# Scores of four heads packed on the rows of the TensorE array, with one exp for the four, in a kernel planned at build time

## The chip, the cores and the metric

The kernel runs on one core of a Trainium2 chip. The metric is the device time of one execution in microseconds (us); three runs of the kernel before took 340.61, 340.77 and 341.06 us, median 340.77. The profile is of one further execution, whose span from first to last instruction is 337.3 us.

## The reference

Two independent computations on bf16 inputs share the launch, and their outputs lie side by side in one result.

- Part A (2048 tokens, 640 channels): a causal convolution of k with four taps, times v, gives kv; kv is convolved along all 2048 tokens with a long filter per channel (by FFT in the reference), `ssm_D * kv` is added, and the sum is multiplied by q.
- Part B (2048 tokens, 640 channels, 32 heads of width 20): attention with a memory, over four segments of 512 tokens.

```python
for s in range(N):                                   # N = 4 segments of L = 512
    logits = einsum('bhqd,bhkd->bhqk', qs, ks) * scale + mask      # causal
    a_dot = einsum('bhqk,bhkd->bhqd', softmax(logits), vs)
    num = einsum('bhld,bhde->bhle', phi(qs), M)      # phi(t) = t + 1 if t > 0 else exp(t)
    den = einsum('bhld,bhd->bhl', phi(qs), z)[..., None] + 1e-06
    outs.append(g * num / den + (1.0 - g) * a_dot)
    M = M + einsum('bhld,bhle->bhde', phi(ks), vs)
    z = z + einsum('bhld->bhd', phi(ks))
```

q, k and v are x times three 640 x 640 weights; the heads' outputs are multiplied by a fourth.

## The kernel before, in words

**Part A** (`a_chunks`) runs five times, for 128 channels each. The long convolution is done as Fourier transforms by matmuls: filter and kv are transformed (`fwd`, banks "a", copied to F by ACT), combined by sums and products on DVE (`bfly`, `pointwise`, `ybfly`: tiles Xh, Kh, S, pr), and transformed back (`inverse`). `kshift` makes the four taps on PE.

**Part B** runs in eight units u: segment s = u // 2, half = u % 2 of 16 heads. `b_proj_chunks` multiplies x by the weights (banks "b"), copies K, Q and V out by ACT, and transposes K and Q by DMA, so that KT and QT hold four heads on the partitions: head hl has rows 32 hl to 32 hl + 19, and a group g of four heads is one slice. Row 32 hl + 20 holds ones in KT and a bound in QT that keeps the exponents small (`bound`). In each token tile of segments 0 to 2, phi of K is made (ACT exp into xm, two DVE ops into PK, lines 714 to 716), and `mem` updates the memory matrix Mbd from PK and V: the product is multiplied by a block mask, its last column by a second factor em (lines 747 and 748), and added (749).

`b_attn_chunks` does the attention. A matmul over 128 rows of KT would mix four heads, so `spread` (line 775) first copies each head's 21 rows of KT by a DMA on the GpSimd queue into KZ, a tile that is zero elsewhere: KZ[:, g, hl] holds head hl on its own rows and zeros on the others. `attn` (782) then goes through a group's heads in two pairs. For each of three specifications of key blocks (block 0; blocks 1 and 3 in one bank; block 2) it makes the scores of both heads, each with 128 rows of KZ against QT, into one "st" bank per head, and ACT takes the exp of each bank into ET: twelve exps a group, of 512, 512 and 256 elements per head. Only queries at or after the key block are computed. DVE multiplies the diagonal blocks by the causal mask in two ops (line 804), PE multiplies ET by V and phi(Q) by Mbd into the "o" bank, in two halves of the queries (805), and DVE divides (820, 827) and adds the two parts into o_s (830), once per half. `outt`, `outproj` and, for the last segment, `out_last` transpose o_s by DMA and multiply by the output weights.

**What sets the order.** All operations are recorded first, with the engine they run on, the PSUM bank they use and their predecessors; a planner (`plan`, `forward`, `backward`, lines 239 to 431) then lays them out by a list schedule with prices written in `price` (182), due times by chunk from two tables of offsets (BIAS, HOLD, from line 879), and hands out the banks: three "st", two "a", two "b", one "o" (878). Every engine gets its instructions in this fixed order (`emit`, line 433), and waits only for what each one needs. So all profile lines carry line 438, the call that emits, and are told apart by their tiles.

Of the kernel before, what the change touches and what calls it, by code (L numbers as in the profile page):

```python
# [26 lines left out]
ET_OFF = {0: 0, 1: 512, 3: 896, 2: 1024}  # L27
# [66 lines left out]
class Recorder:  # L94
# [13 lines left out]
    def bank(self, kind):  # L108
        i = self.turn[kind] % len(self.slots[kind])
        self.turn[kind] += 1  # L110
        t = self.slots[kind][i]
        b = self.home[t[:].tensor.name] = Bank(kind, t[:].tensor.name)
        b.row = kind if kind in ("st", "o") else self.key[0] if kind == "b" and self.key[0] == "P" else None
        if b.row:
            b.seq = self.rows.get(b.row, 0)
            self.rows[b.row] = b.seq + 1
        return t
# [17 lines left out]
    def add(self, eng, method, args, kw):  # L135
# [27 lines left out]
        self.price(op, method, outs[0], ins)  # L163
# [18 lines left out]
    def price(self, op, method, out, ins):  # L182
        n = int(np.prod(list(out.shape)[1:]))
        two = lambda a: mybir.dt.size(a.dtype) == 2
        if method == "matmul":
            op.dur += max(n / 2.4 + 2.5, 27.0)
# [42 lines left out]
    def finish(self):  # L229
        for o in self.ops:  # L230
            o.dur, o.lat = int(round(o.dur)), int(round(o.lat))
            o.dma = None if o.dma is None else int(round(o.dma))
            if o.new and o.bank.kind == "a":
# [213 lines left out]
class K3:  # L447
    def __init__(self, ctx, tc, A_q, A_k, A_v, A_shift_k, A_ssm_k, A_ssm_D, B_x, B_wq, B_wk, B_wv, B_wo, B_beta, out):
# [12 lines left out]
        for kind, n in BANKS.items():  # L461
            self.rec.add_banks(kind, [psum.tile([128, 512], f32, name=f"{kind}{i}") for i in range(n)])
# [37 lines left out]
        self.KQ = [c.tile([128, 2, 16, 32], bf16, name=f"KQ{i}") for i in range(2)]  # L500
# [3 lines left out]
        self.NZ = 2  # L504
        self.KZ = [c.tile([128, 2, 4, L], bf16, name=f"KZ{i}") for i in range(self.NZ)]
        for i in range(self.NZ):
            nc.gpsimd.memset(self.KZ[i][:], 0.0)
        self.PqT = [c.tile([128, 4, L], bf16, name=f"PqT{i}") for i in range(2)]
        self.Mbd = [[c.tile([128, 4, 4, VW], bf16, name=f"Mbd{h}{i}") for i in range(2)] for h in range(2)]
        for i in range(2):  # L510
            nc.gpsimd.memset(self.KQ[i][:, :, :, DH:32], 0.0)
            nc.gpsimd.memset(self.KQ[i][:, 0, :, DH:DH + 1], 1.0)
# [5 lines left out]
    def beta_setup(self):  # L518
# [13 lines left out]
        self.emg = em[:].rearrange("p (g h) -> p g h", h=4)  # L532
# [14 lines left out]
    def a_chunks(self, dp):  # L547
# [13 lines left out]
        def turn(c):  # L561
            def f():
                ps = self.bank("a")
# [23 lines left out]
        def kshift(b):  # L587
            def f():
                kr, vt = st["kr"], st["vt"]
                ps = self.bank("a")  # L590
# [8 lines left out]
        def fwd(kind, c):  # L599
            def f():  # L600
# [3 lines left out]
                for i in range(2):  # L604
                    pf = self.bank("a")
# [28 lines left out]
        def pointwise(b):  # L634
            def f():
# [5 lines left out]
                for i in range(2):  # L641
# [3 lines left out]
                    else:  # L645
                        shp = [128, 2, 8, 128]
                        pr = self.ring("pr", shp)
                        V.tensor_tensor(out=pr[:], in0=Xv[:, i:i + 1, :, 0, :].to_broadcast(shp), in1=Kv[:, :, :, 1, :], op=ALU.mult)
                        V.tensor_tensor(out=Sh[:, i, :, :, 1, :], in0=Sh[:, i, :, :, 1, :], in1=pr[:], op=ALU.add)
# [17 lines left out]
        def inverse(c):  # L667
            def f():
                U, qd = st["U"], st["qd"]
                outa = self.ring("outa", [128, 4, 128], n=2)  # L670
                py = self.bank("a")
# [14 lines left out]
    def b_proj_chunks(self, u):  # L686
# [10 lines left out]
        def proj(tci):  # L697
            def f():
                xT = self.xTs[s]
                tok = slice(128 * tci, 128 * tci + 128)  # L700
                KQ = self.KQ[tci % 2]
                for i in range(3):
                    kq = self.bank("b")
# [4 lines left out]
                if tci == 0:  # L708
                    self.KTs[u] = self.ring("KT", [128, 4, L])
                nc.sync.dma_start_transpose(out=self.KTs[u][:, :, tok], in_=KQ[:, 0, :, :])  # L710
                nc.sync.dma_start_transpose(out=QT[:, :, tok], in_=KQ[:, 1, :, :])
                if s < NS - 1:
                    xm = self.ring("xm", [128, 2, 16, DH])
                    nc.scalar.activation(out=xm[:, 0], in_=KQ[:, 0, :, 0:DH], func=ACTF.Exp)
                    V.tensor_scalar(out=xm[:, 1], in0=KQ[:, 0, :, 0:DH], scalar1=1.0, scalar2=1.0, op0=ALU.add, op1=ALU.max)
                    V.tensor_tensor(out=self.PK[:, tci, :, 0:DH], in0=xm[:, 0], in1=xm[:, 1], op=ALU.min)
            return f

        def bound():
# [11 lines left out]
            pb = self.bank("b")  # L731
# [6 lines left out]
        def mem():  # L738
            src, dst = self.Mbd[half][s % 2], self.Mbd[half][(s + 1) % 2]
            pm = self.bank("b")  # L740
# [5 lines left out]
            mt = self.ring("xm", None)[:].rearrange("p a h d -> p (a h d)")[:, 0:352].rearrange("p (g h e) -> p g h e", g=4, h=4)  # L746
            V.tensor_tensor(out=mt[:, :, :, 0:DH + 1], in0=pmv[:, :, :, 0:DH + 1], in1=self.maskbd[:, None, :, 0:DH + 1].to_broadcast([128, 4, 4, DH + 1]), op=ALU.mult)
            V.tensor_tensor(out=mt[:, :, :, DH], in0=mt[:, :, :, DH], in1=self.emg[:, 4 * half:4 * half + 4, :], op=ALU.mult)
# [12 lines left out]
    def o_pieces(self, s, f0, q0):  # L761
        if s < NS - 1:
            return [(self.o_s[s][:].rearrange("p t h d -> p t (h d)")[:, q0:q0 + 2, f0:f0 + 80], 0, 80)]
        low, high = self.o_parts(s)
        cut = min(max(512 - f0, 0), 80)
        return ([(low[:, q0:q0 + 2, f0:f0 + cut], 0, cut)] if cut else []) + ([(high[:, q0:q0 + 2, f0 + cut - 512:f0 + 80 - 512], cut, 80)] if cut < 80 else [])

    def b_attn_chunks(self, u):
# [6 lines left out]
        def spread(gg):  # L775
            def f():
                for hl in range(4):
                    rows = slice(32 * hl, 32 * hl + DH + 1)
                    nc.gpsimd.dma_start(out=self.KZ[gg][rows, :, hl, :], in_=self.KTs[u][rows, 2 * gg:2 * gg + 2, :])
            return f  # L780

        def attn(g):
            def f():
                KZ = self.KZ[g // 2]
# [3 lines left out]
                ET = self.ring("ET", [128, 4, 1280], n=2)  # L788
                for hp in range(2):
                    for spec in (((0, 0),), ((1, 0), (3, 384)), ((2, 0),)):  # L790
                        sts = [self.bank("st") for j in range(2)]
                        width = 0
                        for j in range(2):
                            hl = 2 * hp + j
                            for (kc, c0) in spec:
                                n = L - 128 * kc
# [209 lines left out]
```

## Time and profile before

| from | what | value |
|---|---|---|
| timed runs | median of three | 340.77 us |
| page, 1 | span | 337.3 us |
| page, 1 | POOL (GpSimd) busy | 77.4 us, 23% |
| groups | scores (all four forms) on PE | 512 matmuls, mean 303 ns, 109.4 us busy |
| groups | exps on ACT | 384, mean 642 ns, 193.4 us busy |
| groups | KZ from KT, issued by POOL | 64 DMAs, 39.6 us busy, 148.8 us idle before |
| waits | POOL for PE st before a KZ copy | 104.6 us in 16 waits |
| page, 3 | DMA queue of POOL (q0) | 7.44 MB, 9.6% of 16 engines' span |

A group's line gives the engine, the operation, what it writes and from what, its shape, the count, then busy time and the mean of one in ns, and behind the second bar the engine's idle time just before these instructions with what ended it. Busy time is a union: where two records of an engine overlap, the time counts once. So a mean is longer than the time after which the next instruction can begin. A busy share near 100% of a stretch says that the engine had little to give there; a share of the whole span mixes start, middle and end.

### The profile page before, as it was taken

How to read it: one execution, taken by the hardware profiler on the slowest of the kernel's cores; microseconds unless marked ns; L12 is line 12 of the kernel's file. 1: busy time of each engine (PE TensorE's matmuls, PEld its weight loads, DVE VectorE, ACT ScalarE, POOL GpSimd, SP SyncE). 2: the span in 40 equal slices, each digit the busy share in tenths (PEclk: the TensorE clock that was granted, in tenths of full speed). 3: DMA queues.
4: the chain of work that ended last, by engine and by line, in shares of the span. 5: the costliest groups of instructions: out<-in, count | busy, mean ns of one | idle time of the engine just before them, and what ended most of it. 6: DMA issues, size and time to landing. Idle time of an engine off the chain costs nothing.

```text
span 337.3 us, 9126 instructions
## 1 busy us (share of the span) xinstructions
PE 303.2 (90%) x3546; PEld 222.1 (66%) x3546; DVE 295.0 (87%) x540; ACT 283.7 (84%) x649; POOL 77.4 (23%) x123
## 2 busy tenths in 40 slices
PE   1998789989998699999997999999989999799882
PEld 1676567648876477878774687777755767566651
DVE  0177999999898999999999899999989998999952
ACT  1857469996998899999999999998998999769911
POOL 9322300241003120233020410340021300822210
PEclk9999799999999799999997999999997999999999
DMA  7986995983259456572475156464330352423153
GB/s 227 251 173 141 182 207 153 180 158 70 48 112 200 74 141 107 95 154 73 77 128 136 35 104 96 71 142 93 76 62 18 85 102 53 100 83 87 52 109 93
DMA packets 100186, 38.34 MB, mean 114 GB/s; under 512 B 92160, under 2 KB 97312, under 8 KB 99888
## 3 DMA queue, kind: packets, MB, share of 16 engines
q1 hardware_dynamic: 94816, 30.01, 45.2%
q0 software_dynamic: 4896, 7.44, 9.6%
q8 instruction: 27, 0.44, 0.5%
q10 hardware_dynamic: 432, 0.34, 0.3%
q14 instruction: 15, 0.12, 0.1%
HBM read 13.36 MB, written 5.24 MB: 55 GB/s over the span
## 4 chain that ended last, share of the span: by engine, by line
PE 60%; ACT 15%; DMA 12%; DVE 9%; issue 4%; SPq 0%; DVEq 0%; ACTq 0%
PE b L438 20%; PE a L438 17%; PE st L438 15%; ACT ET L438 10%; PE o L438 7%; DMA QT<-KQ 6%; DMA kr<-in_A_k_dram 2%; ACT F L438 2%; DMA sk<-in_A_ssm_k_dram 2%; DVE S L438 2%; DVE tq L438 2%; DMA oT<-o_s 1%; DVE ET L438 1%; DVE o L438 1%; ACT KQ L438 1%
## 5 line engine op out<-in xcount | busy, mean ns | idle before, releaser
L438 ACT ACTIVATE ET<-st 128x512 bf16<-128x512 f32 (+1 forms) x384 | 193.4, 642 | 6.8 <-PE st L438 6.1
L438 PE MATMUL st<-QT,KZ 128*128 128x512 bf16 (+3 forms) x512 | 109.4, 303 | 6.1 <-ACT ET L438 5.2
L438 PE MATMUL b<-wqkv,xT 128*128 128x320 bf16 x480 | 79.4, 301 | 0.1
L438 POOL DMA_DIRECT2D KZ<-KT x64 | 39.6, 621 | 148.8 <-PE st L438 104.6
L438 PEld LDWEIGHTS <-KZ 128*128 128x128 bf16 x512 | 45.7, 98 | 27.5 <-issue 12.5
L438 PEld LDWEIGHTS <-xT 128*128 128x128 bf16 x480 | 45.8, 98 | 18.3 <-issue 1.4
L438 ACT CAST F<-a 128x512 bf16<-128x512 f32 x80 | 51.7, 674 | 2.8 <-PE a L438 2.7
L438 PEld LDWEIGHTS <-ET 128*128 128x128 bf16 x1280 | 42.2, 96 | 13.5 <-issue 5.6
L438 PE MATMUL o<-Va,ET 128*128 128x21 bf16 x1280 | 43.9, 173 | 5.8 <-DVE o_s L438 3.4
L438 DVE TENSOR_TENSOR ET<-ET,cmask 128x1024 bf16<-128x1024 bf16 x64 | 42.5, 679 | 1.5 <-ACT ET L438 1.4
L438 PEld LDWEIGHTS <-Wf 128*128 128x128 bf16 x320 | 30.8, 100 | 13.8 <-issue 5.6
L438 ACT CAST KQ<-b 128x320 bf16<-128x320 f32 x64 | 33.7, 526 | 6.9 <-PE b L438 4.0
L438 DVE TENSOR_TENSOR S<-S 128x2048 bf16<-128x2048 bf16 (+1 forms) x40 | 37.3, 945 | 0.1
L438 PE MATMUL a<-kT,Wf 128*128 128x256 bf16 x160 | 26.0, 289 | 0.7 <-ACT F L438 0.6
L438 PE MATMUL b<-wo,oT 128*128 128x320 bf16 (+2 forms) x145 | 23.2, 291 | 1.1 <-DMA oT<-o_s 1.1
L438 PE MATMUL a<-vt,Wf 128*128 128x256 bf16 x160 | 22.8, 272 | 0.9 <-ACT F L438 0.8
L438 DVE TENSOR_TENSOR o<-o,rr 128x320 bf16<-128x320 f32 x48 | 23.2, 483 | 0.2
L438 DVE TENSOR_TENSOR S<-Xh,Kh 128x4096 bf16<-128x4096 bf16 x10 | 22.7, 2274 | 0.0
L438 PE MATMUL a<-skd,kr 128*128 128x128 bf16 x320 | 21.1, 219 | 1.3 <-DMA kr<-in_A_k_dram 1.1
L438 DVE TENSOR_REDUCE kam<-KT 128x4 f32<-128x2048 bf16 x8 | 18.2, 2275 | 4.0 <-DMA KT<-KQ 4.0
L438 PEld LDWEIGHTS <-kr 128*128 128x128 bf16 x320 | 19.3, 98 | 3.1 <-issue 1.7
L438 POOL DMA_DIRECT2D out_dram<-outa x20 | 15.7, 787 | 24.3 <-DVE outa L438 13.7
(68 smaller groups left out, 406.6 us busy)
## 6 DMA issues: line engine op xcount, KB each, us to landing
KZ<-KT POOLq DMA_DIRECT2D x64, 42.0 KB, 2.9
sk<-in_A_ssm_k_dram SPq DMA_DIRECT2D x5, 512.0 KB, 3.9
vt<-in_A_v_dram SPq DMA_DIRECT2D x20, 128.0 KB, 3.7
qd<-in_A_q_dram SPq DMA_DIRECT2D x20, 128.0 KB, 3.0
out_dram<-outa POOLq DMA_DIRECT2D x20, 128.0 KB, 2.9
out_dram<-outb POOLq DMA_DIRECT2D x12, 160.0 KB, 2.1
Wf<-c_wf SPq DMA_DIRECT2D x1, 1024.0 KB
Wi<-c_wi SPq DMA_DIRECT2D x1, 1024.0 KB
```

The source lines that it names most:

```text
L438: f(*[fix(a) for a in args], **{k: fix(v) for k, v in kw.items()})
```

## The change

It replaces the zero-padded K. The four heads of a group have K and Q on their own 32 rows, so four matmuls, each with 32 rows of KT as weights and placed on the array by `tile_position=(32 * hl, 0)`, give the scores of four heads into four PSUM banks. "st" becomes one tile of four banks, and one exp reads all of them. That makes three exps a group (2048, 1536 and 1536 elements; blocks 3 and 2 now share a bank) in the place of twelve. KZ, its memset and `spread` go; KT gets two buffers. The remaining banks are pooled: three "ab" for what "a" and "b" held, and one "o". ET gets a third buffer, and the layout of its blocks is changed so that one DVE op masks all diagonal blocks.

Further edits: phi of K is made for two token tiles at once; the two parts of the output are added once per group instead of once per half; the block mask and em are multiplied once into tables maskE, so `mem` has one op less; the second product of `pointwise` is written over X instead of into tile pr. The planner gets a price for packed matmuls, another rule for the order in which banks are taken, and new BIAS and HOLD tables.

```diff
-ET_OFF = {0: 0, 1: 512, 3: 896, 2: 1024}
+ET_AT = (lambda q: 128 * (3 - q), lambda q: 512 + 128 * (q - 1), lambda q: 896 + 128 * (3 - q), lambda q: 1152)
...
-        b.row = kind if kind in ("st", "o") else self.key[0] if kind == "b" and self.key[0] == "P" else None
+        b.row = kind if kind in ("st", "o") else "P" if self.key[0] == "P" else None
...
         if method == "matmul":
-            op.dur += max(n / 2.4 + 2.5, 27.0)
+            if "tile_position" in kw:
+                op.dur += n / 2.4 * 0.33 + (200.0 if not op.dur else 0.0)
+            else:
+                op.dur += max(n / 2.4 + 2.5, 27.0)
...
-        self.KZ = [c.tile([128, 2, 4, L], bf16, name=f"KZ{i}") for i in range(self.NZ)]
-        for i in range(self.NZ):
-            nc.gpsimd.memset(self.KZ[i][:], 0.0)
...
-                        pr = self.ring("pr", shp)
+                        pr = Xv[:, i].rearrange("p n a r -> p a n r")[:, ::-1]
...
-                if s < NS - 1:
-                    xm = self.ring("xm", [128, 2, 16, DH])
+                if s < NS - 1 and tci % 2 == 1:
+                    xm = self.ring("xm", [128, 2, 2, 16, DH])
+                    K2 = self.KQ[:, :, 0, :, 0:DH]
...
-            V.tensor_tensor(out=mt[:, :, :, DH], in0=mt[:, :, :, DH], in1=self.emg[:, 4 * half:4 * half + 4, :], op=ALU.mult)
...
-        def spread(gg):
-            def f():
-                for hl in range(4):
-                    rows = slice(32 * hl, 32 * hl + DH + 1)
-                    nc.gpsimd.dma_start(out=self.KZ[gg][rows, :, hl, :], in_=self.KTs[u][rows, 2 * gg:2 * gg + 2, :])
-            return f
...
-                ET = self.ring("ET", [128, 4, 1280], n=2)
-                for hp in range(2):
-                    for spec in (((0, 0),), ((1, 0), (3, 384)), ((2, 0),)):
-                        sts = [self.bank("st") for j in range(2)]
...
-                                nc.tensor.matmul(sts[j][:, c0:c0 + n], lhsT=KZ[:, g % 2, hl, 128 * kc:128 * kc + 128], rhs=QT[:, g, 128 * kc:L], start=True, stop=True)
...
-                            nc.scalar.activation(out=ET[:, 2 * hp + j, e0:e0 + width], in_=sts[j][:, 0:width], func=ACTF.Exp, scale=SCALE)
-                for (c0, step) in ((0, 512), (896, 128)):
...
+                ET = self.ring("ET", [128, 4, 1280], n=3)
+                for spec, e0, step in ((((0, 0),), 0, -1), (((1, 0),), 512, 1), (((3, 0), (2, 128)), 896, -1)):
+                    st = self.bank("st")
+                    for (kc, c0) in spec:
+                        for hl in range(4):
+                            rows = slice(32 * hl, 32 * hl + 32)
+                            nc.tensor.matmul(st[:, hl, c0:c0 + L - 128 * kc], lhsT=KT[rows, g, 128 * kc:128 * kc + 128], rhs=QT[rows, g, 128 * kc:L],
+                                             start=True, stop=True, tile_position=(32 * hl, 0))
+                    width = 512 if e0 == 0 else 384
+                    nc.scalar.activation(out=ET[:, :, e0:e0 + width].rearrange("p h (b q) -> p h b q", q=128)[:, :, ::step, :],
+                                         in_=st[:, :, 0:width].rearrange("p h (b q) -> p h b q", q=128), func=ACTF.Exp, scale=SCALE)
+                blk = ET[:].rearrange("p h (i r) -> p (h i) r", i=2)[:, :, 384:640].rearrange("p x (j q) -> p x j q", j=2)
+                V.tensor_tensor(out=blk, in0=blk, in1=self.cmask[:, None, None, :].to_broadcast([128, 8, 2, 128]), op=ALU.mult)
...
-BANKS = {"st": 3, "a": 2, "b": 2, "o": 1}
+BANKS = {"st": (1, 4), "ab": (3, 1), "o": (1, 1)}
```

## The prediction, made before the changed kernel ran

> **What bounds the kernel now.** I read the page's busy times and slices first, then the same busy times over three stretches, to tell a thin start and end from a full middle.
>
> ```profile
> PE 303.2 (90%) x3546; PEld 222.1 (66%) x3546; DVE 295.0 (87%) x540; ACT 283.7 (84%) x649; POOL 77.4 (23%) x123
> DVE  0177999999898999999999899999989998999952
> 0.00:20.00 20.00, 11.80 (x80) 8.30 (x81) 2.37 (x6) 10.74 (x20) 11.66 (x18) 1.00 0.86 225
> 20.00:320.00 300.00, 281.46 (x3339) 207.20 (x3337) 285.54 (x516) 269.82 (x623) 63.95 (x104) 0.98 0.55 107
> 320.00:338.00 18.00, 9.98 (x132) 6.60 (x131) 7.08 (x20) 3.15 (x8) 1.76 (x3) 0.97 0.39 97
> ```
>
> The windows' columns are busy us of PE, PEld, DVE, ACT and POOL. DVE has nearly nothing to do in the first 20 us and works 285.5 of the next 300 (95%). PE has 281.5 (94%) there, ACT 269.8 (90%). So three engines are full at once, and DVE is the fullest. PE's number is the softest, since it counts the modelled ends of matmuls. Next the chain that ended last:
>
> ```profile
> PE 60%; ACT 15%; DMA 12%; DVE 9%; issue 4%; SPq 0%; DVEq 0%; ACTq 0%
> PE b L438 20%; PE a L438 17%; PE st L438 15%; ACT ET L438 10%; PE o L438 7%; DMA QT<-KQ 6%; DMA kr<-in_A_k_dram 2%; ACT F L438 2%; DMA sk<-in_A_ssm_k_dram 2%; DVE S L438 2%; DVE tq L438 2%; DMA oT<-o_s 1%; DVE ET L438 1%; DVE o L438 1%; ACT KQ L438 1%
> ```
>
> The chain runs mostly over PE; scores ("PE st") hold 15%, about 50 us. The copies of K into KZ are not on it. So freeing PE should help, but only until DVE, at 95%, stops it. The groups by form and the answers for tile st give the costs:
>
> ```profile
> L438 ACT ACTIVATE ET<-st 128x512 bf16<-128x512 f32 x256 | 153.7, 714 | 4.7 <-PE st L438 4.3
> L438 ACT ACTIVATE ET<-st 128x256 bf16<-128x256 f32 x128 | 54.5, 499 | 2.2 <-PE st L438 1.8
> L438 PE MATMUL st<-QT,KZ 128*128 128x512 bf16 x128 | 43.1, 385 | 2.4 <-ACT ET L438 2.0
> L438 DVE TENSOR_TENSOR ET<-ET,cmask 128x1024 bf16<-128x1024 bf16 x64 | 42.5, 679 | 1.5 <-ACT ET L438 1.4
> L438 ACT ACTIVATE ET<-st x384: 356/628/1155, 46.0 to 321.3; 128x512 bf16<-128x512 f32 x128, 128x256 bf16<-128x256 f32 x64
> ```
>
> Exps run from 46.0 to 321.3 us. A mean contains a tail in which the next instruction already runs, so I price by start-to-start times in packed stretches of the timeline:
>
> ```profile
> 148.94 1.22 DVE L438 TENSOR_TENSOR F<-F 128x2048 bf16<-128x2048 bf16 x1
> 150.07 0.69 DVE L438 TENSOR_TENSOR Kh<-Kh 128x1024 bf16<-128x1024 bf16 x1
> ...
> 153.40 0.69 DVE L438 TENSOR_TENSOR ET<-ET,cmask 128x1024 bf16<-128x1024 bf16 x1
> 154.00 0.69 DVE L438 TENSOR_TENSOR Kh<-F 128x1024 bf16<-128x1024 bf16 x1
> 154.60 0.24 DVE L438 TENSOR_TENSOR o_s<-o 128x160 bf16<-128x160 bf16 x1
> 154.75 0.23 DVE L438 TENSOR_TENSOR xm<-xm,em 128x16 bf16<-128x16 bf16 x1
> 155.02 0.35 DVE L438 TENSOR_TENSOR Mbd<-Mbd,xm 128x336 bf16<-128x336 bf16 x1
> 164.43 2.06 ACT L438 ACTIVATE ET<-st 128x512 bf16<-128x512 f32 x4
> ```
>
> On DVE 2048 elements take 1.13 us, a mask 0.60, an o_s add 0.15, the product with em 0.27 because the next op needs its result. So a mask has only some 0.06 us of fixed cost. On ACT four exps of 512 take 2.06, so with a last record of 0.60 (the exp at 316.56) each is (2.06 - 0.60)/3 = 0.48; two of 256 (163.40, together 0.66, one being 0.39) give 0.27; PqT's 2048 elements take 1.81 (177.30 to 179.11).
>
> **What the Trainium skill says.** "TensorE: Matmul & The Clock Gate", Part 3 on row and column tiling: four matmuls of 32 rows, 512 columns, on different row groups were measured at 3.07 times the speed of one after the other; no run here shows it yet. "TensorEngine Tiling (Array Packing)", Key Properties: changing the tiling mode drains TensorE, with no price given. "ScalarE: Activation LUTs", What ACT_TABLE_LOAD costs: about 0.83 ns per element for every function plus a fixed part, of which neighbours overlap some. The trace agrees on the slope: (0.48 - 0.27)/256 = 0.82 ns. "VectorE: DVE Perf Modes", the tier table: bf16 tensor_tensor runs at most two elements a cycle, so merging two such ops saves only the fixed part; the trace agrees (0.60 and 1.13 for 1024 and 2048).
>
> **The change, part by part.**
>
> PE. Five matmuls of 320 columns take 0.84 us (155.70, in full), the last 0.30: 0.135 each, 0.42 ns a column. A head's scores are 512+384+256+128 = 1280 columns, 0.54 us; 128 head groups make 69 us. At 3.07 times this is 23. Added is the change of mode: the order of the changed kernel has 188 changes, each between 0 and about 0.17 us (what a matmul's record exceeds its streaming by: 0.38 - 0.21 for 512 columns), so 0 to 32 us; I take half, 16. PE saves 69 - 23 - 16 = 30 us, between 14 and 46. All lies on the path until DVE takes over.
>
> ACT. A group of four heads costs 4 x (2 x 0.48 + 0.27) = 4.9 us in twelve exps, and 1.81 + 2 x 1.38 (1536 elements by the slope) = 4.6 in three: 0.3 x 32 = 10 us less. Phi of K in pairs saves 1 us, two copies for the mask tables add 0.8. ACT saves 10 us, beside DVE work.
>
> DVE. Masks: 64 x 0.60 = 38.4 become 32 x 1.13 = 36.2, saving 2.2. Phi of K: 24 pairs of ops (0.15 + 0.24 in packed stretches) become 12 of twice the size (0.23 + 0.40), saving 1.8. Sums into o_s: 48 x 0.15 become 24 x 0.23, saving 1.7. The six products with em, 0.27 each, go: 1.6; the mask tables add 0.3. Together 7 us. The product that used tile pr now overwrites X in the same form: 0.
>
> Others at nothing. The 64 copies into KZ and its memset on POOL are off the chain, hidden by the exps before them. Their 2.7 MB also leave the DMA engines; in the head, where those are 86% busy, only eight copies of 42 KB had been issued, a microsecond at most.
>
> Added wait. The four st banks are one buffer. Each pack of scores waits for the exp of the pack before, and that exp for its four matmuls. Behind a waiting score matmul stand PE's projections and transforms in fixed order; behind a waiting exp stand ACT's casts, and DVE waits for those. One turn is: an exp's tail, 0.12; its end to the released matmul, 0.05 (179.11 + 0.58 to 179.74); the pack, 0.38 to 0.5; its end to the exp, 0.04 (316.52 to 316.56). That is 0.7 us, plus whatever stands on PE at that moment (a projection's five matmuls are 0.7). The order of the changed kernel puts other ACT work of 90 us, at the prices above, into the 95 gaps: none in 6, one instruction in 17, two or more in 72. Taking each gap as the longer of its filling and the turn, first to last exp needs 245 us at a turn of 0.7, 262 at 1.1, 277 at 1.3, 293 at 1.5. Before the first exp stand 46 us and after the last 16, as now, so at 0.7 to 1.1 the exps end the kernel at 307 to 324 us of span and hardly bind.
>
> **Sum.** DVE: 295.0 - 7 = 288 us of work. Its idle time is 337.3 - 295.0 = 42.3: 17.6 in the first 20 us, 10.2 in the last 17.3, 14.5 between. Start and end stay: first scores come after 280 matmuls instead of 288, and the end is the same transposes and output projection. Of the middle's idle time I let PE's relief remove about half, to 8. Span: 288 + 17.6 + 10.2 + 8 = 324. The timed runs exceed the profiled span by 340.8 - 337.3 = 3.5, so 327 us.
>
> **Rivals.** (1) DVE's gaps close further and the ends shrink: middle 3, head 4 and end 2 less, 313 of span, 316 us. For it: PE is 60% of the chain. Against: the head is loads and transposes. (2) The single st buffer becomes the bound: with 0.7 us of other matmuls in front of each pack the turn is 1.4, the exps need 285, span 46 + 285 + 16 = 347, 350 us. For it: three buffers become one, and PE's order is fixed in advance. Against: 72 of 95 gaps have filling. (3) The turn is about 1.3 and eats what was gained: 277 + 62 = 339, 342 us, no gain.
>
> **Numbers.** Forecast 0.58, rival one 0.20, two 0.15, three 0.07 (of which 0.04 within 0.2% and 0.03 slower). So faster 0.78, same 0.04, slower 0.18. The range takes in rival one and part of three: 315 to 339.
>
> **What would show it.** DVE at 93% or more from 20 us on and near 288 us busy; ACT near 274; score packs of about 0.28 us streaming; the KZ rows gone. Wrong would be: exps that wait for "PE st" by tens of microseconds, packs longer than 0.6 us, or DVE idle for casts in the middle.

## The result and the profile after

The changed kernel takes 335.59 us (median of 4 runs, 335.43 to 337.54) beside 340.91 us of the kernel before: ratio 0.986, 95% interval 0.981 to 0.991. A second measurement, the control of the experiments below, gave 0.985 (0.980 to 0.990). Some executions fall into a slower state (here one of the kernel before, 347.32 us); ratios leave them out, and the table below leaves out the busy and idle times of a profile that fell into it. So it is faster by 1.4%, where 4% was forecast: the time lies inside the range, the gain is about a third of the forecast one.

First the page's busy times of the changed kernel, the slices of DVE and of the granted TensorE clock, and three stretches cut as in the prediction (busy us of PE, PEld, DVE, ACT, POOL, then the clock, the DMA share and GB/s):

```profile
PE 274.4 (82%) x3544; PEld 192.2 (58%) x3546; DVE 286.8 (86%) x455; ACT 265.2 (79%) x351; POOL 29.8 (9%) x57
DVE  0057899999799889999989988999999989999942
PEclk9999599999979998999979996999959999997698
0.00:20.00 20.00, 11.67 (x98) 9.41 (x99) 1.51 (x3) 10.23 (x19) 4.43 (x16) 1.00 0.91 230
20.00:320.00 300.00, 256.40 (x3398) 179.22 (x3397) 281.51 (x444) 253.38 (x328) 24.63 (x41) 0.93 0.48 99
320.00:334.00 14.00, 6.28 (x59) 3.58 (x56) 3.73 (x8) 1.60 (x4) 0.75 (x1) 0.92 0.39 95
```

All three engines lost work: PE 28.8 us, ACT 18.5, DVE 8.2. But in the 300 us of the middle DVE works 281.5 where it worked 285.5, so its idle time there rose from 14.5 to 18.5 us. Over the whole span, which doesn't depend on where the middle is cut, it rose from 337.3 - 295.0 = 42.3 to 333.7 - 286.8 = 46.9. The clock row differs from that of the kernel before:

```profile
PEclk9999799999999799999997999999997999999999
```

There 7 stands five times, in the changed kernel 5, 6 and 7 stand seven times, and the mean clock fell from 0.979 to 0.936. Next the chain that ended last, by engine and by line:

```profile
DVE 36%; PE 33%; ACT 15%; DMA 8%; issue 5%; SPq 2%; DVEq 0%; ACTq 0%
PE ab L441 26%; DVE S L441 11%; ACT ET L441 7%; DVE ET L441 6%; DVE Xh L441 4%; PE o L441 4%; PE st L441 3%; DMA QT<-KQ 3%; ACT F L441 3%; DVE outa L441 2%; DVE o L441 2%; DVE kam L441 2%; ACT PqT L441 2%; SPq L441 2%; DMA ident<-c_ident 2%
```

The scores went from 15% of the chain to 3%, and DVE took over a large part of it, yet the chain is only 1% shorter. The groups by form, with busy us, mean ns and the idle time ahead:

```profile
L441 ACT ACTIVATE ET<-st 128x1536 bf16<-128x1536 f32 x64 | 94.9, 1483 | 9.8 <-PE st L441 9.6
L441 ACT ACTIVATE ET<-st 128x2048 bf16<-128x2048 f32 x32 | 61.5, 1921 | 2.9 <-PE st L441 2.9
L441 PE MATMUL st<-QT,KT 32*128 32x512 bf16 x128 | 13.0, 393 | 4.0 <-ACT ET L441 3.8
L441 PE MATMUL st<-QT,KT 32*128 32x384 bf16 x128 | 11.3, 341 | 4.8 <-ACT ET L441 4.8
L441 DVE TENSOR_TENSOR ET<-ET,cmask 128x2048 bf16<-128x2048 bf16 x32 | 38.7, 1208 | 1.6 <-ACT ET L441 1.5
```

The score matmuls of 512 columns hold 13.0 us where they held 43.1. The two lines on the exps show 12.5 us of waits for scores, those on the scores 8.6 us of waits for exps (17.5 with the 128-column form, which isn't shown). Scores are not the only place where PE waits now. First the kernel before, then the changed one: the matmuls into the "o" bank, and the longest waits of DVE for PE:

```profile
L438 PE MATMUL o<-Va,ET 128*128 128x21 bf16 x1280 | 43.9, 173 | 5.8 <-DVE o_s L438 3.4
DVE rr L438 <- PE o L438: 3.6, 6, 1.7
DVE vt L438 <- PE a L438: 1.2, 2, 1.0
```

```profile
L441 PE MATMUL o<-Va,ET 128*128 128x21 bf16 x1280 | 44.3, 173 | 17.4 <-DVE o L441 9.3
DVE rr L441 <- PE o L441: 5.7, 8, 1.1
DVE outa L441 <- PE ab L441: 4.2, 3, 2.9
DVE vt L441 <- PE ab L441: 3.9, 5, 1.3
```

A wait's line gives us in all, times, and the longest. PE idles 17.4 us ahead of these matmuls where it idled 5.8, for 9.3 of them until DVE has read the one "o" bank, and DVE in turn waits longer for PE. So part of what PE gained it stands idle for. And this is a pack of four matmuls in the timeline (start, length, engine, operation):

```profile
152.46 0.71 PE L441 MATMUL ab<-wqkv,xT 128*128 128x320 bf16 x4
153.10 0.34 PE L441 MATMUL st<-QT,KT 32*128 32x384 bf16 x4
153.38 0.45 PE L441 MATMUL ab<-wqkv,xT 128*128 128x320 bf16 x2
153.50 1.45 ACT L441 ACTIVATE ET<-st 128x1536 bf16<-128x1536 f32 x1
```

The four projections ahead stream for 4 x 0.135 = 0.54 us, to 153.00; the pack starts 0.10 later, its four matmuls within 0.010 us, and the next projection starts 0.28 after it. One stream of 384 columns is 0.16 us, so 0.10 us goes ahead of the pack and 0.12 behind it.

### The profile page after: what moved, and what is told of

The parts are those of the page before. It is cut to its first block, busy times and chain, and to the rows that moved or that the text cites. A ratio compares the mean times of both kernels' runs of the same rounds, so it can differ in the third digit from the quotient of the medians.

```text
span 333.7 us, 8539 instructions
## 1 busy us (share of the span) xinstructions
PE 274.4 (82%) x3544; PEld 192.2 (58%) x3546; DVE 286.8 (86%) x455; ACT 265.2 (79%) x351; POOL 29.8 (9%) x57
## 4 chain that ended last, share of the span: by engine, by line
DVE 36%; PE 33%; ACT 15%; DMA 8%; issue 5%; SPq 2%; DVEq 0%; ACTq 0%
PE ab L441 26%; DVE S L441 11%; ACT ET L441 7%; DVE ET L441 6%; DVE Xh L441 4%; PE o L441 4%; PE st L441 3%; DMA QT<-KQ 3%; ACT F L441 3%; DVE outa L441 2%; DVE o L441 2%; DVE kam L441 2%; ACT PqT L441 2%; SPq L441 2%; DMA ident<-c_ident 2%
## 5 line engine op out<-in xcount | busy, mean ns | idle before, releaser
L441 ACT ACTIVATE ET<-st 128x1536 bf16<-128x1536 f32 (+1 forms) x96 | 156.4, 1629 | 12.8 <-PE st L441 12.5
L441 PE MATMUL ab<-wqkv,xT 128*128 128x320 bf16 x480 | 75.9, 302 | 2.3 <-DVE outa L441 0.8
L441 PE MATMUL o<-Va,ET 128*128 128x21 bf16 x1280 | 44.3, 173 | 17.4 <-DVE o L441 9.3
L441 PE MATMUL st<-QT,KT 32*128 32x128 bf16 (+3 forms) x512 | 35.8, 312 | 18.1 <-ACT ET L441 17.5
L441 ACT CAST F<-ab 128x512 bf16<-128x512 f32 x80 | 44.9, 625 | 6.2 <-PE ab L441 5.7
L441 DVE TENSOR_TENSOR ET<-ET,cmask 128x2048 bf16<-128x2048 bf16 x32 | 38.7, 1208 | 1.6 <-ACT ET L441 1.5
L441 PEld LDWEIGHTS <-Wf 128*128 128x128 bf16 x320 | 29.8, 101 | 13.6 <-issue 7.9
L441 ACT CAST KQ<-ab 128x320 bf16<-128x320 f32 x64 | 27.9, 466 | 10.1 <-issue 5.0
L441 PE MATMUL ab<-skd,kr 128*128 128x128 bf16 x320 | 23.7, 233 | 2.1 <-DMA kr<-in_A_k_dram 2.1
L441 PE MATMUL ab<-kT,Wf 128*128 128x256 bf16 x160 | 23.9, 283 | 1.4 <-ACT kT L441 1.0
L441 PE MATMUL ab<-vt,Wf 128*128 128x256 bf16 x160 | 23.1, 285 | 0.8 <-ACT KQ L441 0.5
L441 PE MATMUL ab<-wo,oT 128*128 128x320 bf16 (+1 forms) x140 | 22.1, 300 | 0.5 <-DVE outa L441 0.5
L441 DVE TENSOR_REDUCE kam<-KT 128x4 f32<-128x2048 bf16 x8 | 18.2, 2275 | 3.3 <-DMA KT<-KQ 1.8
```

Of the source, the lines that this page charges most:

```text
L441: f(*[fix(a) for a in args], **{k: fix(v) for k, v in kw.items()})
```

## The experiments

Theories, as the expectations name them: A, VectorE alone is the bound; B, the single score buffer; C, the half clock; D, the path runs over all engines in turn and each one's work counts for a part of its length; E, several engines are nearly full and the next takes over; F, the bank that projections and transforms lost; G, no harm by the banks. Unless said otherwise an edit keeps the changed kernel's order of instructions and acts only where they are emitted. Ratios are to the kernel before, with 95% intervals; us are ratios times 341. "Less" in a name is what was left out, as the sum of its records or of its streaming time; the third column has what the page's busy time really fell by (from the control, or from the kernel before), which is less. "Idle" is the span less DVE's busy time. The control lost 29.8 us of PE, 8.6 of DVE and 18.3 of ACT against the kernel before.

| kernel | ratio | busy time that fell | idle of DVE |
|---|---|---|---|
| before | 1 | | 42.3 |
| changed, as control | 0.985 (0.980 to 0.990) | | 46.1 |
| changed, DVE less 39 us | 0.961 (0.955 to 0.966) | DVE 32.3 | 71.2 |
| changed, PE less 32 us | 0.977 (0.972 to 0.982) | PE 22.7 | 45.0 |
| changed, ACT less 32 us | 0.972 (0.966 to 0.978) | ACT 28.0 | 42.8 |
| changed, all three | 0.918 (0.912 to 0.924) | PE 28.4, DVE 34.6, ACT 31.8 | 58.0 |
| before, DVE less 43 us | 0.998 (0.995 to 1.000) | DVE 32.6 | 77.5 |
| before, PE less 32 us | 0.990 (0.987 to 0.993) | PE 18.6 | 40.2 |
| before, PE less 32, DVE less 8 | 0.986 (0.978 to 0.994) | | |
| before, PE less 32, DVE less 8, ACT less 18.5 | 0.979 (0.975 to 0.984) | PE 25.0, DVE 6.9, ACT 14.3 | 44.0 |

**The control.** The changed kernel itself, beside the three runs on the changed kernel that relieve PE, relieve ACT and fill its gaps.

> The changed kernel itself, as the control beside the runs that follow. All theories: 0.984 to 0.987 of the kernel before, 335 to 337 us where the kernel before takes 341.

It gave 0.985, as expected; its median is 337.05 us beside 341.7.

**What a microsecond of each engine is worth in the changed kernel.**

```
# masks left out
+ if method == "tensor_tensor" and "cmask" in kw["in1"].tensor.name: continue
# PE less
+ calls = calls[:2] + [(*calls[2][:3], {**calls[2][3], "stop": True})]   # for wqkv and wo
# ACT less
+ kw = {**kw, "out": kw["out"][:, 0:3], "in_": kw["in_"][:, 0:3]}        # the score exps
```

> The changed kernel in its own order, with the 32 causal-mask products on Vector left out (so the diagonal blocks are not masked). Vector loses 32 x 1.13 = 36 us of work and the output matmuls follow the exps directly. Theory A: Vector is 94% busy from 20 to 320 us, so the time falls by 25 to 36 us, to 300 to 311. Theories B and C: PE and ACT, held up at the score buffer or by the clock, set the time soon after, and it falls by less than 15 us, to 321 or more.

> The changed kernel's own order, with 32 us of TensorE left out: the projections to q, k, v and the output projection of the first three segments sum over three of five chunks, 240 of their matmuls of 135 ns are gone. Theory A (VectorE alone is the bound): within 2 us of the changed kernel. Theory D (no engine alone sets the time; each one's work counts for about a quarter of its length, as the 36 us less of VectorE that gave 8 to 9): 5 to 10 us faster. Theory C (clock): at most 3 us faster or even slower, as TensorE streams less and more windows fall to half clock, 5 or more of them beyond those of the changed kernel.

> The changed kernel's own order, with some 32 us of ScalarE left out: 87 of the 96 score exps cover three heads of four (the fourth head's weights are old ones). Theory A (VectorE alone is the bound): within 2 us of the changed kernel. Theory B (the single score buffer: TensorE waits until the exp has read it): 15 us faster or more, since every turn of the buffer is 0.3 to 0.45 us shorter. Theory D (shared between the engines): 5 to 12 us faster.

> The changed kernel's own order, with all three cuts at once: mask products left out (VectorE, 39 us), three of five chunks summed in the projections (TensorE, 32 us), three heads of four in 87 of the exps (ScalarE, 32 us). Alone they gave 8, 3 and 6 us. If each engine is held by the others because all three are nearly equally busy (theory E: the next busiest takes over as soon as one is relieved), the three together give far more than the sum of 17, some 25 to 32 us. If the rest of the time is latency, transfers and half clock in a fixed order (theory D), they give about the sum, 14 to 20 us.

Against the changed kernel's 0.985 the cuts give 8.4 us for 39 of DVE, 2.7 for 32 of PE and 4.6 for 32 of ACT; together 22.7, more than the sum of 15.7. Theory A falls: an engine that alone sets the time would have given its whole cut until the next one binds, and the others nothing. Theory B had expected 15 us or more of the shorter exps. What the cut of DVE turned into is in its waits:

```profile
DVE rr L443 <- PE o L443: 16.2, 24, 1.9
DVE kam L443 <- DMA KT<-KQ: 8.0, 5, 2.2
DVE outa L443 <- PE ab L443: 7.0, 4, 3.7
DVE vt L443 <- PE ab L443: 5.4, 8, 1.3
```

In the changed kernel these four are 5.7, 1.8, 4.2 and 3.9. DVE gets to its next instruction sooner and waits there for PE or a transpose. D and E both hold in part: each engine counts for 8 to 22% of its cut, or 12 to 26% of what its busy time fell by, and the three are tied to each other, since freeing all gives more than one by one (between what D and what E expected).

**The same cuts in the kernel before.** Here the edits act in the old order with the old eight banks.

> The kernel before, its own order, with the 64 products of the causal mask left out (43 us of VectorE; the weights above the diagonal stay). Theory A (VectorE alone is the bound, as the prediction took it): the time falls until TensorE's 284 us bind, by 5 to 15 us at least and more if the idle time of VectorE closes too. Theory D: 6 to 12 us faster, ratio 0.965 to 0.982, VectorE idle by 30 us more in waits for TensorE and for the K transposes.

> The kernel before, its own order, with the same 32 us of TensorE left out as in the run on the changed kernel (the projections to q, k, v and the output projection of the first three segments sum over three of five chunks, 240 matmuls of 135 ns are gone). It asks what relief of TensorE alone is worth where TensorE is 84% busy. Theory A (VectorE alone is the bound): within 2 us of 341. Theory D (each engine's work counts for a part of its length, more where it is busier): 5 to 10 us faster, ratio 0.97 to 0.985. Theory C (the time taken off TensorE returns as half clock): several more half-clock windows than the five of before, and at most 4 us faster.

The windows from 20 to 320 us, first without masks, then with PE relieved, and the wait that grew in the first:

```profile
20.00:320.00 300.00, 278.88 (x3302) 205.05 (x3301) 251.01 (x449) 266.24 (x615) 62.89 (x101) 0.97 0.55 106
DVE rr L440 <- PE o L440: 25.9, 31, 2.2
```

```profile
20.00:320.00 300.00, 266.49 (x3166) 187.93 (x3164) 288.58 (x527) 268.31 (x624) 64.55 (x104) 0.98 0.57 109
```

Leaving out the masks of DVE, the engine that the forecast called the bound, is worth 0.2% (0 to 0.5%): its busy time fell by 32.6 us, its idle time grew by 35.2, and the reads of the o bank alone now wait 25.9 us for PE where it was 3.6. That is less than A and D expected; only D's 30 us more of idle time came. 32 us less of PE is worth 1.0%, or 3.3 us, between A and D; DVE's idle time fell only from 42.3 to 40.2. Theory C had allowed for several more half-clock windows; the clock stayed at 0.977 and the gain was small all the same.

To see what the change's three lighter loads are worth together, the kernel before then got them by leaving work out:

```
+ if masks % 5 == 0: continue        # 12 of the 64 mask products
+ if exps % 9 == 0: continue         # 37 of the 384 score exps (second run only)
```

> The kernel before with its own order and its eight banks (three for scores, two and two for projections and transforms, one for outputs), from which the change's relief of TensorE and VectorE is taken by leaving work out: 32 us of TensorE (the projections sum over three of five chunks) and 12 of the 64 mask products, 8 us of VectorE. Theory F (the loads are worth what the forecast said, and the changed kernel gives part back through its three shared banks): 8 us below the kernel with only TensorE relieved (0.9903), that is 0.966 to 0.974, 328 to 332 us. Theory G (the loads are worth no more than the changed kernel shows, with any banks): 0.982 to 0.990, 334.5 to 337.5 us.

> As the run before, with 37 of the 384 score exps left out as well (18.5 us of ScalarE, as much as the change took), so that all three engines carry the changed kernel's load in the old order and the old banks. Theory F: 0.955 to 0.972, 325 to 331 us, VectorE's idle time in the middle at 9 to 12 us against 18 of the changed kernel. Theory G: 0.980 to 0.990.

The first gave 0.986 with a wide interval, as G expected, the second 0.979 (0.975 to 0.984), between what F and G expected and next to G. Its busy times and its window:

```profile
PE 278.2 (84%) x3306; PEld 197.8 (60%) x3306; DVE 288.1 (87%) x528; ACT 269.4 (81%) x612; POOL 77.4 (23%) x123
20.00:320.00 300.00, 262.50 (x3196) 187.49 (x3194) 282.08 (x515) 256.97 (x587) 65.04 (x104) 0.98 0.56 109
```

DVE works 282.1 us and idles 17.9 there, nearly the changed kernel's 281.5 and 18.5, with the old buffers, the old order and a clock of 0.98. So lighter loads alone leave DVE idle about as long as the change does. Over the span DVE's idle time is 40.2 us with PE relieved and 44.0 with DVE and ACT relieved as well: of the 6.4 us that DVE's busy time fell by between the two, 3.8 are found again as idle time. Two limits belong to this run. Its loads stay 1 to 4 us above those of the changed kernel, and the work is left out at other places: PE is relieved in the projections, not in the scores. So it is a likeness of the change, not the change itself.

**The packing undone.** The four heads' matmuls all go to the first 32 rows and can't run at once:

```
+ kw["tile_position"] = (0, 0)      # lhsT and rhs moved to partitions 0 to 31
```

> The changed kernel's own order, with the matmuls of the four heads all put on the first 32 rows (the scores of heads 1 to 3 are those of head 0): what is undone is that the four run at once. TensorE then streams the scores in 69 us in place of 17, some 52 us more. Theory A with TensorE behind it: TensorE's busy time goes from 274 to some 320 us less what the warmer clock gives back (some 10 us), and the time to 355 to 375 us. Theory D (a tenth to a quarter of the added length counts): 341 to 350 us. Theory C: few half-clock windows are left.

Ratio 1.077 (1.069 to 1.085), 31 us slower than the changed kernel, within what theory A with PE behind it gave (some 367 us). The page and a wait:

```profile
PE 328.9 (90%) x3546; PEld 218.7 (60%) x3546; DVE 290.4 (79%) x455; ACT 271.2 (74%) x351; POOL 30.2 (8%) x57
ACT ET L448 <- PE st L448: 40.9, 60, 2.7
```

PE holds 54.5 us more, near the estimate. The price of PE's time isn't symmetric: 54.5 us more of its busy time cost 31 us, 22.7 less gave 2.7. The expected warmer clock did not come; it was 0.923.

**The single score buffer.** One run halves it in the fixed order: two tiles of two banks, each with an exp of two heads, so that PE may refill the first half while ACT reads the second. Another makes scores for pairs of heads in two buffers that take turns, and lets the planner order everything anew, with tables fitted by a search.

```
+ for h, part in ((slice(0, 2), low), (slice(2, 4), high)):
+     f(*args, **{**kw, "out": kw["out"][:, h], "in_": part})
# pairs
-BANKS = {"st": (1, 4), "ab": (3, 1), "o": (1, 1)}
+BANKS = {"st": (2, 2), "ab": (3, 1), "o": (1, 1)}
```

> The changed kernel, in its own order of instructions on every engine, but the four score banks are two tiles of two banks and each exp is two, over heads 0-1 and 2-3, so that the next pack's first half can start half an exp earlier and ACT's first half need not wait for PE's second. Theory B (the single score buffer stops PE and ACT): the waits of score matmuls for exps (18.7 us) and of exps for score matmuls (12.5 us) fall to under 10 us together, Vector's idle time between 20 and 320 us falls from 18.5 to about 12, and the time falls by 4 to 8 us, to 328 to 332. Theory A (Vector's own work is the bound, its remaining idle time has many small causes): no more than 1 us either way, since 96 more exps cost ACT about 8 us beside Vector's work. Theory C (PE's clock at half speed takes back what was freed): as A, unless fewer windows of half clock follow.

> The changed kernel with its scores made for two heads at a time, into two buffers of two banks that take turns (192 exps of two heads in place of 96 of four), ordered anew by the planner, which knows of the two buffers, with fitted tables. Theory B (the single score buffer of four banks is the loss, and an order laid for one buffer could not show it): 326 to 332 us. Theory F (the three shared banks are the loss, and they stay): 333 to 340 us, VectorE's idle time in the middle still at 16 to 20 us.

The halves gave 0.985 (0.982 to 0.989), no change, though the waits did move. First the changed kernel, then the halves:

```profile
PE st L441 <- ACT ET L441: 18.7, 20, 4.2
ACT ET L441 <- PE st L441: 12.5, 17, 1.7
```

```profile
ACT ET L452 <- PE sthigh L454: 10.7, 14, 1.5
PE st L454 <- ACT ET L452: 6.8, 4, 3.4
PE sthigh L454 <- ACT ET L452: 4.9, 14, 0.6
```

PE waits 7 us less for exps and the time stays, though the 96 exps more also cost ACT 4.7 us. The pairs gave 1.003 (1.000 to 1.005), slower than the changed kernel and than both B and F expected; their new order may be part of that, so they say little of the buffer. Theory B is not supported: that PE has these waits to spare is the likely reading, not a shown one.

**The longest of these waits.** At unit boundaries PqT's exp, which waits for a transpose, stands ahead of a score exp:

```profile
163.75 0.34 PE L441 MATMUL st<-QT,KT 32*128 32x128 bf16 x8
163.77 1.91 ACT L441 ACTIVATE PqT<-QT 128x2048 bf16<-128x2048 bf16 x1 [0.45 <-DMA QT<-KQ]
165.58 1.43 ACT L441 ACTIVATE ET<-st 128x1536 bf16<-128x1536 f32 x1
167.06 0.40 PE L441 MATMUL st<-QT,KT 32*128 32x512 bf16 x4 [2.98 <-ACT ET L441]
```

PE stands still for 2.98 us. The edit puts each of the six PqT exps behind the next score exp:

```
+ order.insert(min(j, use - 1), order.pop(i))    # i: a PqT exp, j: the next score exp on ACT
```

> The changed kernel with one move: each of the six exps of Q for phi (1.9 us, waiting for the transposed Q) goes behind the next score exp in ACT's order. It stands in front of that score exp now, while PE waits for the score buffer (2.98 us at 164.1, 4.16 us at 196.0), and after those idle stretches the clock is at half for 3.4 to 6.8 us. Theory C: three or four of the eleven windows of half clock go, and the time falls by 3 to 6 us, to 330 to 332. Theory B: the idle stretches at the score buffer go, 2 to 4 us. Theory A: no more than 1 us.

Ratio 0.993 (0.990 to 0.996), 2.8 us slower than the changed kernel. None of the theories expected a loss. PE's wait fell from 18.7 to 12.3 us, but ACT's waits for scores rose from 12.5 to 18.2, and DVE now waited 5.9 us for PqT where it was 1.1. A wait of PE was traded for waits of ACT and DVE.

**The banks.** The changed kernel has three banks for projections and transforms, the kernel before had two and two. One run takes a further one from the changed kernel and orders it anew, but with the tables that were fitted to three banks. Two runs give the kernel before three or four that both kinds share, each ordered anew with tables fitted by a search.

```
-BANKS = {"st": (1, 4), "ab": (3, 1), "o": (1, 1)}
+BANKS = {"st": (1, 4), "ab": (2, 1), "o": (1, 1)}
# the kernel before
-BANKS = {"st": 3, "a": 2, "b": 2, "o": 1}
+BANKS = {"st": 3, "ab": 3, "o": 1}          # and 4, as the control
```

> The changed kernel with two banks in the place of three for projections and transforms, planned anew by the same tables; the eighth bank is free. It is the base for a run that keeps the clock up with matmuls into the free bank. Theory A: at most 5 us slower than the changed kernel, since PE and ACT have room and Vector sets the time. Theory B: 5 to 15 us slower, since PE has one place less to work ahead while scores wait. Theory C: slower by as much as the number of half-clock windows rises, about 1 us for each.

> The kernel before with its four projection and transform banks (two of each) cut to three that both share, as in the changed kernel; the three score banks stay, the eighth bank is unused. The planner orders it anew, with its bias and hold tables fitted by a search. Theory F (what the changed kernel loses is the fourth of these banks: operations queue for a bank, and VectorE waits for TensorE's results): slower than the same kernel with four shared banks by 4 us or more, and VectorE's waits for TensorE's ab and o banks rise from the 3 us of before to some 6 to 10. Theory G (the number of banks does no harm from four to three; the order does): within 2 us of it.

> The control to the run with three shared banks: four shared banks in place of two and two, ordered and fitted in the same way. Theory F and G: 341 to 347 us, near the kernel before, since no bank is taken; VectorE's waits for TensorE's banks stay at some 3 us.

Two banks in the changed kernel gave 1.085 (1.080 to 1.089), 34 us more, beyond what any theory expected; how much of it is the bank and how much the tables that were not fitted was not separated. ACT's casts wait for PE and DVE for o:

```profile
DVE rr L441 <- PE o L441: 15.5, 19, 1.6
ACT KQ L441 <- PE ab L441: 14.5, 18, 2.0
```

In the kernel before three shared banks gave 1.039 (1.033 to 1.045), four gave 1.012 (1.007 to 1.017): a bank is worth some 9 us there. But four shared banks take nothing away and still cost 1.2%, so a new order alone moves the time by several us, and part of the 9 may be the order too. Time agrees with theory F, its waits don't: DVE's grew at ACT's casts (one of 8.3 us for F), not at PE's banks. And the run with the lighter loads says that in the changed kernel F is at most a remainder: 0.979 with the old banks against 0.985, intervals that overlap.

**The half clock.** 42 matmuls that compute nothing fill nine gaps of PE, alone and together with the half exps:

```
+ for _ in range(fill[o.idx]):      # 3 to 8, ahead of nine operations
+     self.real.tensor.matmul(self.slots[kind][i][:, 0:512], lhsT=self.filler[:, 0, 0, 0:128], rhs=self.filler[:, 0, 1, :], start=True, stop=True)
```

> The changed kernel's own order, with 42 matmuls of 512 columns that compute nothing put in front of nine operations at which TensorE had stood idle for 0.8 to 2.3 us while a bank was free (five of them in the last 35 us, where three windows of 3.4 us at half clock lie). Theory C (what the change took off TensorE came back as half clock, because TensorE streams too little ahead of these windows): the half-clock windows at 304 to 315 us go, some 5 us of clock come back, and the time falls by 2 to 6 us, to 330 to 334. Theory A (VectorE is the bound) and theory D (the engines wait for each other in turn and no one of them sets the time): the windows may go, but the time stays within 1.5 us, or rises by up to 3 us as the filling matmuls run past the gaps.

> The changed kernel's own order, with both the two half exps on two score tiles and the 42 filling matmuls: the two edits that alone gave 0.9852 and 0.9781 of the kernel before, against 0.9851 of the changed kernel. If the clock and the single buffer are each worth a little: 331 to 334 us, ratio 0.970 to 0.978. If neither is (theory F): 334 to 337 us, ratio 0.980 to 0.987.

Alone they gave 0.978 (0.972 to 0.984), with an interval that overlaps the changed kernel's; beside the control, measured in the same session, the means differ by 2.4 us (0.5 to 4.3), the low end of what C expected. Together with the half exps they gave 0.985 (0.980 to 0.989), what F expected. The clock row of the second:

```profile
PEclk9999899999999998999979995999999999999998
```

The mean clock over its six runs is 0.963 where the control's six have 0.933: some 10 us of clock come back, (0.963 - 0.933) x 333, and the time stays. So in this order the half clock doesn't hold the missing gain. A gain of 2 us or so from the filled gaps is possible, but the two runs don't agree on it, and it isn't shown.

## Why the prediction was wrong

**PE's saving: right in sum.** A pack enters and leaves with 0.10 to 0.12 us each; 188 changes make 19 to 22 us, and 32 groups of 1280 columns stream for 17. PE's scores take 36 to 39 us in place of 69; 30 to 33 saved where 30 was forecast. There is some luck in it: the four matmuls of a pack stream fully at once, so the stream is 17 us where 3.07 times gave 23, and the changes are dearer than the 16 that were taken, half of a bound. The two errors go against each other. The page's PE fell by 28.8, at a lower clock.

**ACT's and DVE's work: right for DVE, low for ACT.** DVE went from 295.0 to 286.8, 8.2 less where 7 was worked out. ACT went from 283.7 to 265.2, 18.5 less where 10 was worked out. That some of it is tails of exps, which a page counts as busy, is likely but was not separated.

**The edits at nothing** held: the KZ rows are gone, and the start idles 18.5 us where 17.6 was taken, the end 13.7 - 3.7 = 10.0 where 10.2 was.

**The added wait** was priced well enough: exps wait 12.5 us for scores, not the tens that would have been wrong, and the run with half exps speaks against its being on the path. Rivals two and three fall with it, and rival one's closing gaps did not come.

**The signs.** DVE at 93% or more held (281.5 of 300 is 94%), as did packs of 0.28 us and exps that hardly wait. They could not tell the forecast from the result: 94% leaves 18 us of idle time, and the forecast's 8 us would have been 97%.

**The sum: here it failed.** The step is "Of the middle's idle time I let PE's relief remove about half, to 8". It measured 18.5. The rest of the sum holds: 286.8 of work, 18.5 idle at the start, 10.0 at the end make 315.3, with 18.5 in the middle 333.8 of span. The timed runs exceed the profiled span by 1.9 where 3.5 was taken, so 335.7. (The 3.5 set the median of the timed runs against the span of another execution, which itself took 339.53 us, 2.2 above its span.) With 8 us in the middle it would have been some 325.

Behind this step stands another, "freeing PE should help, but only until DVE, at 95%, stops it", read as if DVE's work and its idle time were two terms that may each be lowered. In the kernel before, relief of PE alone lowered DVE's idle time by 2.1 us of 42.3, where the forecast took off 6.5. And taking work off DVE mostly lengthened its idle time, since DVE's next operand comes when PE, ACT or a transpose delivers it: leaving out the masks gave 0.2%, and lighter loads on all three engines in the old buffers gave 2.1% with 44.0 us of idle time. The 7 us that the sum credited to DVE were worth little; the forecast counted them in full. The chain that the prediction shows had said as much of DVE, with 9% of the span and 1% at the masks. Its 60% for PE, though, promised more than the 1.0% that 32 us less of PE gave.

What stays open: whether the changed kernel loses anything to its three shared banks, its order or its clock. The difference of 0.979 and 0.985 would be 2 us, less than these intervals tell. Open too is what two "o" banks would do, for which PE and DVE wait on each other; it was not tested. Nor was a fourth bank for projections and transforms in the changed kernel: with four for scores, three for these and one for o, all eight that both kernels use are given out.

## What to carry to other kernels

In this kernel three engines were busy for 90 to 95% of the same stretch, fed in fixed order, and none of them was the bound: the highest share did not say what a microsecond less is worth, and idle time was no reserve that another engine's relief could be credited with. So before adding up savings of two engines, leave the work out in the old kernel and time it. Here the run without masks would have told that DVE's microseconds were worth next to nothing, and the one with lighter loads the gain to within 0.7%. Compare idle time over the whole span, as a fixed window reaches further into the thin end of a shorter run. A bank given to one use is taken from another, and it pays to measure what that one is worth, with the order fitted anew.

## What the runs showed of the hardware that was not expected

Four matmuls on four groups of 32 rows start within 0.010 us and stream at once. Yet a pack of 512 columns takes 0.42 us, 0.10 on entry and the rest from its start to the next matmul, against 4 x 0.216 = 0.86 one after the other (start to start in the run with one row group): twice as fast where it stands between full-array matmuls. The Trainium skill has 3.07 times for four such matmuls ("TensorE: Matmul & The Clock Gate", Part 3, on row tiling); what decides here is the measurement, 4 for the stream alone and 2 with entry and exit. The by-form rows of the kernel with one row group add up to 34.7 + 27.6 + 21.1 + 13.3 = 96.7 us of scores, those of the changed kernel to 13.0 + 11.3 + 9.6 + 7.8 = 41.7.

The half clock comes without idle windows. The same page, Part 1, has the clock fall to half after an idle window of some 3.4 us, and knows of a kernel whose frequent short idle times do it too, without a level. The traces show half-clock stretches of 3.41 us and multiples, one from 34.9 to 41.7 us in the changed kernel, but TensorE was idle all through the window ahead of them in only 4 of 123 cases.

A level can be worked out from the traces. Cut each run into windows of 3.41 us in step with its clock changes. In each, add up the columns streamed (0.42 ns each, twice that at half clock), weighted by the share of the 128 rows that a matmul uses, and divide by the window. Over all twenty kept profiles, without the first 8 us and the last two windows, that gives:

| clock in this window and the next | windows | share streamed |
|---|---|---|
| full, then half | 123 | at most 0.38 |
| full, then full | 1583 | at least 0.33 |
| half, then full | 120 | at least 0.70 |
| half, then half | 67 | at most 0.76 |

So in these runs the clock fell after a window with less than about a third to 0.38 streamed, and it came back only after one with 0.70 to 0.76 or more. The weight matters where 32 rows stream alone. In the run with one row group, windows of up to 0.46 without it were followed by half clock, and windows of up to 0.90 stayed in it; with it these are 0.35 and 0.74, as in the other runs. So PE was 90% busy there and its clock was 0.923.

A relief of TensorE can thus be paid in part with clock: 32 us taken off the changed kernel's PE lowered its mean clock over six runs from 0.933 to 0.912, which is 7 us at 332 us of span. In the kernel before, the same cut left it nearly where it was (0.979 and 0.977 in the two profiles).
